# Attention interleaved with a feed-forward: two key chunks per visit, three banks for the dense products

## The chip, the cores and the metric

The kernel runs on one core of one Trainium2 chip. A core has five engines with queues of their own: TensorE (PE, matrix products into PSUM; its weight loads are listed as PEld), VectorE (DVE), ScalarE (ACT), GpSimd (POOL) and SyncE (SP), which here only issues DMA. Each queue is worked off in order; engines wait for one another through semaphores. PSUM has eight banks, and a matrix product writes into one of them until another engine has read it. The metric is the time of one execution on the device, in microseconds, the median of several runs.

## The reference

Attention with normalized queries and keys (8 batches, 12 heads, 448 positions, head width 64), then a feed-forward with squared ReLU over all 3584 tokens (width 768, inner width 2048), everything in float32:

```python
q_n, k_n = rmsnorm(q, g_q), rmsnorm(k, g_k)
scores = q_n @ k_n.T / sqrt(64)
attn = exp(scores - max);  attn = attn / (sum(attn) + 1e-9)
x = (attn @ v) rearranged to (batch * 448, 12 * 64)
h = maximum(x @ w_in, 0)
out = (h * h) @ w_out
```

## The kernel before, in words

**Attention.** Work goes by pairs of heads, 48 of them (`pairs`, six per batch). For a pair, `load_qk` and `load_v` fetch queries, keys and values, `square` (ScalarE) and `normalize` (VectorE, GpSimd) give the norms, and `turn` transposes the queries (x = 0) and keys (x = 1) on TensorE (L181) and copies them out of PSUM with VectorE or ScalarE. The keys are cut into four chunks of 112 (`NJ = 4`). `weigh(i, m)` makes the scores of chunk m for both heads (L202; one head on each half of the array's rows) and ScalarE takes the exponentials (L204). Since the exponentials are bounded, no maximum is taken off. `attend(i, m)` multiplies weights and values (L262; one head on each half of the array's columns). The denominators are products with ones: for the twelve first pairs (`alone`) a product per chunk (L269), later one product of the weights summed by GpSimd and VectorE (`add_up`, L217 and L220; the product is L273). A reciprocal (L284) and a multiplication in `finish` (L294) give the pair's output, kept in SBUF.

**Feed-forward.** It goes by units of two batches (`ffn(u)`, u = 0 to 3). Both matrix products use a form of Strassen's scheme: seven products of half-size blocks, P1 to P7, instead of eight (`PRODUCTS`, with the bank each takes, the two forms it multiplies, and whether it starts the bank). `make_x_forms` makes the sums of inputs, `make_weight_forms` and `make_sums` those of weights. A unit has four blocks. A block has two sets of first products (`first_products`, L392; seven products of six passes each), whose results are combined on VectorE (L412), passed through ReLU and square on ScalarE (L413, L414) and kept as hidden tiles; then, in `second_products`, the rows shared by the two batches (L441), sums of hidden tiles (L435), and three groups of seven second products (L458; four passes each), which VectorE adds into accumulators (L491, L475; in the first block ScalarE copies them, L489 and L473). A float32 matmul appears as two records, here called passes.

**Banks.** Four banks (4 to 7) take the feed-forward's products in turn (`roles`, `turn_roles`); a product that takes over a bank waits until the earlier one has been read. The attention has the other four; the first pair of each unit (`between`) uses some of the feed-forward's too.

**Order.** The order of every queue is written out by hand: instructions of each engine run in program order (`manual_schedule`). Pairs 0 to 11 run without feed-forward. From then on, `ffn(u - 1)` is a generator that yields after each product with a cost, and the main loop (L662 to L698) takes as many products before each chunk of attention as keep the two in proportion. A unit's first pair runs alone; the products are spread over the chunks of the eleven others. So each chunk of a pair is a *visit* of the attention between dense products: scores of chunk n for this pair, values of chunk n for the pair before.

**Weights.** They come as 64-bit words that are converted on the way, in pieces, by ScalarE (`split_words`) and VectorE (`join_words`, L569 to L581). Sixteen pieces (`early`) are converted in the first stage, the others (`late`) during the first unit's feed-forward, one per `COST_IN` of cost, tied to the products by `convert`. The finished forms are written to DRAM and loaded again for later units (`load_in`, `load_out`).

The words of the code that the change turns on are these:

```python
FIRST_ORDER = ["P1", "P5", "P6", "P4", "P3", "P7", "P2"]
SECOND_ORDER = ["P1", "P5", "P2", "P6", "P4", "P3", "P7"]
roles = list(banks[4:8])
COST_IN, COST_OUT = 12 * NK // 2, 10
```

Of the kernel before, what the change touches and what calls it, by code (L numbers as in the profile page):

```python
# [74 lines left out]
def program(ctx, tc, q, k, v, g_row, moe_w_in, moe_w_out, out, shift):  # L75
# [40 lines left out]
    weights, sums, dens, xts, forms = {}, {}, {}, {}, {}  # L116

# [3 lines left out]

    def between(i):

        return pairs[i][0] % 2 == 0 and pairs[i][1] == 0
# [50 lines left out]
    def turn(i, x):  # L175

        rows = normal[i][0][x]
        tr = banks[2 + x if alone(max(i - 1, 0)) else 2][:, 0:S]
        dst = att.tile([P, S], F32, name="qT" if x == 0 else "kT")
        for j in range(NJ):  # L180
            nc.tensor.transpose(tr[:, ts(j, CP)], rows[:, j].rearrange("p h d -> p (h d)"), ident[:CP, :CP])  # L181
        if x == 0:
            nc.vector.tensor_scalar(out=dst, in0=tr, scalar1=g, scalar2=None, op0=ALU.mult)  # L183
        else:
            nc.scalar.copy(dst, tr)  # L185
        turned[i, x] = dst

    def new_weights(i, m):
        for e in range(2):
            weights[i, e, m] = att.tile([CP, S], F32, name="wT", tag="wT", bufs=2 * NJ + 2)  # L190

    def weigh(i, m):
# [5 lines left out]
        odd = (2, 3) if alone(i) else (4, 6) if between(i) else (0, 1)  # L198
        scs = [banks[odd[e] if m % 2 else e][:CP, 0:S] for e in range(2)]
# [7 lines left out]
        add_up(i, m)  # L207

    def add_up(i, m):

        if m < 2 or alone(i):
            return
        for e in range(2):
            engine = nc.gpsimd if e == 0 else nc.vector
            if m == 2:
                sums[i, e] = att.tile([CP, S], F32, name="sum", tag="sum", bufs=2)
                engine.tensor_tensor(  # L217
                    out=sums[i, e], in0=weights[i, e, 0], in1=weights[i, e, 1], op=ALU.add
                )
            engine.tensor_tensor(out=sums[i, e], in0=sums[i, e], in1=weights[i, e, m], op=ALU.add)  # L220

    def weigh_shifted(i, m):
# [18 lines left out]
        if m == NJ - 1:  # L241
            for n in range(NJ):
                add_up(i, n)

    def values_bank(i):
        apart = i < last and between(i + 1)
        return banks[4 + i % 2 if alone(i) else 5 if apart else 3][:, 0:S]

    def sums_bank(i):
        apart = i < last and between(i + 1)  # L250
        return banks[6 + i % 2 if alone(i) else 7 if apart else 2][:, 0:S]

    def attend(i, m):

        av = values_bank(i)
        den = sums_bank(i)  # L260
# [5 lines left out]
        for e in range(2):  # L266
            wT = weights.pop((i, e, m))
            if alone(i):
                nc.tensor.matmul(  # L269
                    den[ds(e * D, D), :], lhsT=ones, rhs=wT, start=m == 0, stop=m == NJ - 1  # L270
                )
            elif m == 1:
                nc.tensor.matmul(  # L273
                    den[ds(e * D, D), :], lhsT=ones, rhs=sums.pop((i, e)), start=True, stop=True
                )
        if m == (NJ - 1 if alone(i) else 1):
            rden = new_x()
            if shift:
                nc.vector.tensor_scalar(
                    out=rden, in0=den, scalar1=1e-9, scalar2=None, op0=ALU.add  # L280
                )
                nc.vector.reciprocal(out=rden, in_=rden)
            else:
                nc.vector.reciprocal(out=rden, in_=den)  # L284
            dens[i] = rden
# [4 lines left out]
    def finish(i):  # L290
# [8 lines left out]
        if b % 2 and c >= NK:  # L299
            make_x_forms(b // 2, c - NK)  # L300
# [44 lines left out]
    roles = list(banks[4:8])  # L345

    def turn_roles(order):

        x, v_, w, y = roles
        roles[:] = (y, v_, w, x) if order is FIRST_ORDER else (w, y, v_, x)  # L350

# [3 lines left out]
        "P4": (3, True, "22", "T4"), "P5": (1, True, "S1", "T1"), "P6": (0, False, "S2", "T2"),  # L355
# [3 lines left out]
    FIRST_ORDER = ["P1", "P5", "P6", "P4", "P3", "P7", "P2"]  # L359
    SECOND_ORDER = ["P1", "P5", "P2", "P6", "P4", "P3", "P7"]  # L360
# [3 lines left out]
    def ffn(u):  # L364
# [5 lines left out]
        for blk in range(NBLK):  # L370
# [4 lines left out]
            for t in range(2):  # L375
                yield from first_products(u, 2 * blk + t, [a[:, t] for a in hid])
            yield from second_products(u, blk, hid, accs)
# [5 lines left out]
    def first_products(u, p, hid):  # L383
# [4 lines left out]
        for name in FIRST_ORDER:  # L388
# [8 lines left out]
            if name in ("P1", "P5", "P6", "P4"):  # L397
                copies[name] = ffn_p.tile([P, S], F32, name="part", tag="part", bufs=4)
                nc.scalar.copy(copies[name], ps)  # L399
            elif name == "P2":  # L400
                hidden(hid[0][:, 0], ps, copies["P1"], ALU.add)
                load_in(n + 2)
            elif name == "P3":
                hidden(hid[0][:, 1], ps, copies["P6"], ALU.add)
            elif name == "P7":
                hidden(hid[1][:, 0], ps, copies["P4"], ALU.subtract)
                hidden(hid[1][:, 1], ps, copies["P5"], ALU.add)
            yield COST_IN
        turn_roles(FIRST_ORDER)

    def hidden(dst, ps, part, op):
        nc.vector.tensor_tensor(out=dst, in0=ps, in1=part, op=op)  # L412
# [3 lines left out]
    def second_products(u, blk, hid, accs):  # L416
# [14 lines left out]
        for engine, dst, left, right, op in (  # L431
            (nc.vector, s1, a21, a22, ALU.add), (nc.vector, s2, s1, a11, ALU.subtract),
            (nc.gpsimd, s4, a12, s2, ALU.subtract), (nc.gpsimd, s3, a11, a21, ALU.subtract),
        ):
            engine.tensor_tensor(out=dst, in0=left, in1=right, op=op)  # L435

        for half in range(2):
            ps = roles[half][:, 0:HALF]
            for a in (1, 0):
                for t in range(2):  # L440
                    nc.tensor.matmul(  # L441
                        ps, lhsT=flat[a][:, t, ds(FULL, P)], rhs=w_sb[t][:, 2 * a + half, :],
                        start=a == 1 and t == 0, stop=a == 0 and t == 1,
                    )
            add_to(accs[-1][:, ts(half, HALF)], ps, blk == 0)
            yield 2 * COST_OUT
        turn_roles(SECOND_ORDER)

        lefts = {"11": a11, "12": a12, "22": a22, "S1": s1, "S2": s2, "S3": s3, "S4": s4}
        for tt in range(NT):  # L450
# [31 lines left out]
            turn_roles(SECOND_ORDER)  # L482
# [150 lines left out]
    late = deque(conversions(2, product + 2 * COST_IN, COST_IN))  # L633
    for blk in range(1, NBLK):
        late.extend(conversions(4 if blk < NBLK - 1 else 2, blk * block + 1, COST_IN))
# [15 lines left out]
    unit_steps = 2 * NPAIR * NJ  # L651

    with tc.manual_schedule(engines=ENGINES):
# [7 lines left out]
        stream, spent = iter(()), 0  # L661
        for i, (b, c) in enumerate(pairs):  # L662
            u = b // 2
            for n in range(NJ):
                step = (b % 2) * NPAIR * NJ + c * NJ + n
                if n == 0:
                    if i > 1 and not shift:
                        finish(i - 2)
                    load_v(i)
                if n == NJ - 1 and i + 3 <= last:  # L670
                    load_qk(i + 3)
                if step == NJ and u:
                    stream, spent = ffn(u - 1), 0
                while u and (
                    shift and step == NJ and spent < COST
                    or spent * (unit_steps - NJ) < COST * (step - NJ + 1)
                ):
                    spent += next(stream)
                    while u == 1 and late and late[0][0] <= spent:
                        convert(late.popleft()[1])  # L680
                if n == 2 and i + 2 <= last:
                    normalize(i + 2)
                if shift and n == 0 and i:
                    for m in range(NJ):
                        attend(i - 1, m)
                    finish(i - 1)
                weigh(i, n)
                if i and not shift:
# [49 lines left out]
```

## Time and profile before

| | |
|---|---|
| median of 3 runs | 1588.81 us (1587.44 to 1589.5) |
| profiled execution | 1587.84 us, span of its instructions 1586.0 us |
| TensorE busy | 1523.8 us, 5204 passes |
| VectorE busy | 821.0 us |
| ScalarE busy | 622.0 us |
| GpSimd busy | 454.3 us |
| mean granted TensorE clock | 0.991 |
| reciprocal, VectorE | 48, mean 2957 ns |
| exponential, ScalarE | 384, mean 628 ns |
| addition into an accumulator, VectorE | 324, mean 551 ns |

A line of the profile names an engine, a line of the kernel (L392), an operation and its tiles, out<-in. Busy time of TensorE is pipelined: a pass is listed for 543 ns while the next one starts before it ends, so times between starts are what counts. A line of the windows view gives a stretch of the span, its length, and the busy time of each engine in it. A line of the waits view says which engine at which line waited for which other, with the total, the number and the longest, in us.

### The profile page before, as it was taken

The numbers are of one execution on the slowest core, as the hardware profiler recorded it, in microseconds if no ns is written. First come the engines' busy times: TensorE is split into PE (matmuls) and PEld (weight loads), VectorE is DVE, ScalarE is ACT, GpSimd is POOL, SyncE is SP. The second block draws the span as 40 slices with busy tenths as digits, with TensorE's granted clock in tenths as the row PEclk, the third lists the DMA queues.
The fourth block names the chain that finished last, engine by engine and source line by source line (L and its number), as shares of the span: only waits on it lengthen the run. The fifth ranks groups of instructions, "written<-read, shape, count | busy, mean of one in ns | idle before, by whom it ended". The sixth has DMA issues, their size and how long they took to land.

```text
span 1586.0 us, 15000 instructions
## 1 busy us (share of the span) xinstructions
PE 1523.8 (96%) x5204; PEld 703.3 (44%) x5204; DVE 821.0 (52%) x1234; ACT 622.0 (39%) x1161; POOL 454.3 (29%) x298
## 2 busy tenths in 40 slices
PE   5999999899799999999999999999999999999997
PEld 2333444344344444444444444444444444555554
DVE  3887485977958654345363563345444452223323
ACT  4775464726527244341433334343332412231130
POOL 3445433332423353322132333223231221000000
PEclk9999999999999999999999999999999999999999
DMA  4555143533525152230313242132222205222122
GB/s 103 158 148 169 32 130 97 197 118 92 185 84 182 53 184 92 74 123 18 132 55 125 74 148 89 52 132 62 101 92 97 69 13 184 78 106 106 43 80 72
DMA packets 131801, 164.65 MB, mean 104 GB/s; under 512 B 92804, under 2 KB 115844, under 8 KB 123524
## 3 DMA queue, kind: packets, MB, share of 16 engines
q1 hardware_dynamic: 131712, 163.60, 31.6%
q8 instruction: 43, 0.70, 0.2%
q14 instruction: 42, 0.34, 0.1%
q10 hardware_dynamic: 4, 0.00, 0.0%
HBM read 128.98 MB, written 34.60 MB: 103 GB/s over the span
## 4 chain that ended last, share of the span: by engine, by line
PE 89%; DVE 5%; ACT 4%; issue 1%; POOL 0%; DMA 0%; POOLq 0%; ACTq 0%; DVEq 0%
PE bank L392 29%; PE bank L458 28%; PE bank L202 11%; PE bank L262 10%; PE bank L441 4%; PE bank L181 3%; PE bank L269 2%; PE bank L273 2%; DVE xT L284 1%; ACT hid L414 1%; ACT hid L413 1%; DVE sum L220 1%; ACT wT L204 1%; DVE hid L412 1%; DVE in_sb L607 0%
## 5 line engine op out<-in xcount | busy, mean ns | idle before, releaser
L392 PE MATMUL bank<-xT,in_sb 128*128 128x448 f32 x1344 | 522.9, 543 | 2.5 <-DVE xT L294 2.5
L204 ACT ACTIVATE wT<-bank,rr 112x448 f32<-112x448 f32 x384 | 221.3, 628 | 392.4 <-PE bank L202 386.8
L392 PEld LDWEIGHTS bank<-xT,in_sb 128*128 128x128 f32 x1344 | 249.2, 190 | 252.2 <-issue 235.3
L164 POOL TENSOR_TENSOR rr<-ms,minus_half 112x16 f32<-112x16 f32 x48 | 151.0, 3145 | 567.1 <-DVE ms L160 561.8
L458 PE MATMUL bank<-out_sb,hid 128*128 128x384 f32 x768 | 277.0, 490 | 9.0 <-DVE acc L491 9.0
L491 DVE TENSOR_TENSOR acc<-acc,bank 128x384 f32<-128x384 f32 x324 | 173.2, 551 | 186.8 <-PE bank L458 155.1
L458 PE MATMUL bank<-out_sb,sums 128*128 128x384 f32 x576 | 212.4, 491 | 0.0
L284 DVE RECIPROCAL xT<-bank 128x448 f32<-128x448 f32 x48 | 141.9, 2957 | 117.3 <-PE bank L273 99.2
L202 PE MATMUL bank<-qT,kT 64*112 64x448 f32 x768 | 199.8, 595 | 1.6 <-ACT kT L185 0.6
L458 PEld LDWEIGHTS bank<-out_sb,hid 128*128 128x128 f32 x768 | 145.2, 191 | 113.3 <-DVE acc L491 10.3
L262 PE MATMUL bank<-wT,vt 112*64 112x448 f32 x768 | 188.3, 570 | 2.9 <-DVE xT L294 2.9
L399 ACT COPY part<-bank 128x448 f32<-128x448 f32 x128 | 68.0, 531 | 255.9 <-PE bank L392 255.8
L412 DVE TENSOR_TENSOR hid<-bank,part 128x448 f32<-128x448 f32 x128 | 76.2, 616 | 174.6 <-PE bank L392 171.9
L458 PEld LDWEIGHTS bank<-out_sb,sums 128*128 128x128 f32 x576 | 105.6, 190 | 81.9 <-issue 13.4
L413 ACT ACTIVATE hid<-hid 128x448 f32<-128x448 f32 x128 | 73.3, 572 | 135.4 <-DVE hid L412 135.4
L220 DVE TENSOR_TENSOR sum<-sum,wT 112x448 f32<-112x448 f32 x72 | 65.4, 909 | 116.5 <-ACT wT L204 114.1
L435 POOL TENSOR_TENSOR sums<-hid,sums 128x768 f32<-128x768 f32 x16 | 29.3, 1829 | 298.6 <-PE bank L441 182.1
L220 POOL TENSOR_TENSOR sum<-sum,wT 112x448 f32<-112x448 f32 x72 | 86.5, 1201 | 87.1 <-ACT wT L204 83.8
L441 PE MATMUL bank<-out_sb,hid 128*128 128x384 f32 x256 | 93.2, 508 | 16.0 <-ACT hid L414 16.0
L202 PEld LDWEIGHTS bank<-qT,kT 64*112 64x112 f32 x768 | 55.6, 175 | 114.4 <-issue 58.8
L262 PEld LDWEIGHTS bank<-wT,vt 112*64 112x64 f32 x768 | 38.6, 136 | 132.1 <-issue 117.7
L183 DVE TENSOR_SCALAR qT<-bank,g 128x448 f32<-128x448 f32 x48 | 32.7, 682 | 95.8 <-PE bank L181 95.8
(53 smaller groups left out, 1084.1 us busy)
## 6 DMA issues: line engine op xcount, KB each, us to landing
out_sb<-out_forms SPq DMA_DIRECT2D x24, 1536.0 KB, 8.1
in_sb<-in_forms SPq DMA_DIRECT2D x24, 1344.0 KB, 5.7
words<-in_moe_w_in_dram SPq DMA_DIRECT2D x32, 384.0 KB, 3.6
words<-in_moe_w_out_dram SPq DMA_DIRECT2D x32, 384.0 KB, 3.2
out_forms<-out_sb SPq DMA_DIRECT2D x8, 1536.0 KB, 6.7
qk<-in_q_dram SPq DMA_DIRECT2D x96, 112.0 KB, 2.9
qk<-in_k_dram SPq DMA_DIRECT2D x96, 112.0 KB, 3.0
vt<-in_v_dram SPq DMA_DIRECT2D x48, 224.0 KB, 2.8
```

Of the source, the lines that this page charges most:

```text
L164: nc.gpsimd.tensor_tensor(out=rr.rearrange("p x r -> p (x r)"), in0=ms, in1=minus_half.to_broadcast([CP, 4 * NJ]), op=ALU.pow,)
L202: nc.tensor.matmul(sc, lhsT=kT[r, ts(m, CP)], rhs=qT[r, :], start=True, stop=True)
L204: nc.scalar.activation(weights[i, e, m], sc, AF.Exp, scale=normal[i][1][:, 2 * m + e : 2 * m + e + 1])
L220: engine.tensor_tensor(out=sums[i, e], in0=sums[i, e], in1=weights[i, e, m], op=ALU.add)
L262: nc.tensor.matmul(av[ds(e * D, D), :], lhsT=values[i][:, e, m, :], rhs=weights[i, e, m], start=m == 0, stop=m == NJ - 1,)
L284: nc.vector.reciprocal(out=rden, in_=den)
L392: nc.tensor.matmul(ps, lhsT=w_sb[:, IN.index(left), c, :], rhs=forms[u, c][right], start=first and c == 0, stop=c == NK - 1, skip_group_ch ...
L412: nc.vector.tensor_tensor(out=dst, in0=ps, in1=part, op=op)
L413: nc.scalar.activation(dst, dst, AF.Relu)
L441: nc.tensor.matmul(ps, lhsT=flat[a][:, t, ds(FULL, P)], rhs=w_sb[t][:, 2 * a + half, :], start=a == 1 and t == 0, stop=a == 0 and t == 1,)
L458: nc.tensor.matmul(ps, lhsT=lefts[left][:, t, ts(tt, P)], rhs=w_sb[t][:, OUT.index(right), :], start=first and t == 0, stop=t == 1, skip_g ...
L491: nc.vector.tensor_tensor(out=acc, in0=acc, in1=ps, op=ALU.add)
```

## The change

- A pair is visited twice instead of four times, each time for two chunks: in the first visit of pair i the values of pair i - 1 for chunks 0 and 1 and the scores of pair i for chunks 0 and 1, in the second the rest. The values come first now. The denominators' product stands at the start of the second visit and is copied out of PSUM by ScalarE; the reciprocal then works on the copy in SBUF. Scores take banks 0 to 3.
- The transposes of `turn` stand halfway between two visits, in bank 0. In the stage before the feed-forward they take, of the two banks each that values and denominators have in turn, those not in use.
- VectorE's work for the attention (reciprocal, `finish`, sums, norms) goes into a list, `tasks`, of which one is issued after each product.
- The feed-forward has three banks (5 to 7) instead of four. The orders of the products are new; P4 comes last in the first products, and P7's copy is taken from PSUM and P4 subtracted from it.
- The shared rows are multiplied in two parts: three of the four factors for both halves, then the sums of hidden tiles are issued, then the last factor.
- All twelve pairs of a unit, its first one included, are spread over the feed-forward of the unit before, in 24 equal steps: the scores of the next unit's first pair are made in the last steps. The x forms are made when those of the unit before have been used (`complete`). In the old order the last pair's values came after the last spread product; now they are spread too.
- Late conversions come every `2 * COST_OUT` (20) instead of every `COST_IN` (18). The weights' buffers are 8 instead of 10, those of the sums 4 instead of 2.

```diff
@@ def turn
-        tr = banks[2 + x if alone(max(i - 1, 0)) else 2][:, 0:S]
+        tr = banks[6 - 2 * x + (i - 1) % 2 if i < 2 or alone(i - 2) else 0][:, 0:S]
@@ def weigh
-        odd = (2, 3) if alone(i) else (4, 6) if between(i) else (0, 1)
-        scs = [banks[odd[e] if m % 2 else e][:CP, 0:S] for e in range(2)]
+        scs = [banks[m % 2 * 2 + e][:CP, 0:S] for e in range(2)]
...
-        add_up(i, m)
@@ instead of the end of attend
+    def denominators(i):
+        den = sums_bank(i)
+        for e in range(2):
+            nc.tensor.matmul(
+                den[ds(e * D, D), :], lhsT=ones, rhs=sums.pop((i, e)), start=True, stop=True
+            )
+        dens[i] = new_x()
+        nc.scalar.copy(dens[i], den)
+
+    def invert(i):
...
+        nc.vector.reciprocal(out=dens[i], in_=den)
@@ feed-forward
-    roles = list(banks[4:8])
+    roles = list(banks[5:8])
...
-        "P4": (3, True, "22", "T4"), "P5": (1, True, "S1", "T1"), "P6": (0, False, "S2", "T2"),
+        "P4": (2, True, "22", "T4"), "P5": (1, True, "S1", "T1"), "P6": (0, False, "S2", "T2"),
...
-    FIRST_ORDER = ["P1", "P5", "P6", "P4", "P3", "P7", "P2"]
-    SECOND_ORDER = ["P1", "P5", "P2", "P6", "P4", "P3", "P7"]
+    FIRST_ORDER = ["P1", "P5", "P2", "P6", "P3", "P7", "P4"]
+    SECOND_ORDER = ["P1", "P2", "P5", "P6", "P3", "P4", "P7"]
@@ def first_products
-            if name in ("P1", "P5", "P6", "P4"):
+            if name in ("P1", "P5", "P6", "P7"):
...
-                hidden(hid[1][:, 0], ps, copies["P4"], ALU.subtract)
                 hidden(hid[1][:, 1], ps, copies["P5"], ALU.add)
+            elif name == "P4":
+                hidden(hid[1][:, 0], copies["P7"], ps, ALU.subtract)
+                load_in(n + 2)
@@ def second_products
+        parts = [(0, 0), (1, 0), (0, 1), (1, 1)]
+        for some in (parts[:3], parts[3:]):
+            for half in range(2):
+                ps = roles[half][:, 0:HALF]
+                for a, t in some:
                     nc.tensor.matmul(
                         ps, lhsT=flat[a][:, t, ds(FULL, P)], rhs=w_sb[t][:, 2 * a + half, :],
-                        start=a == 1 and t == 0, stop=a == 0 and t == 1,
+                        start=(a, t) == parts[0], stop=(a, t) == parts[-1],
                     )
...
+            if some[-1] != parts[-1]:
+                for engine, dst, left, right, op in (
+                    (nc.vector, s1, a21, a22, ALU.add), (nc.vector, s2, s1, a11, ALU.subtract),
+                    (nc.gpsimd, s4, a12, s2, ALU.subtract), (nc.gpsimd, s3, a11, a21, ALU.subtract),
+                ):
+                    engine.tensor_tensor(out=dst, in0=left, in1=right, op=op)
@@ order
+    def run(until):
+        nonlocal spent
+        while spent < until:
+            spent += next(stream)
+            while first and late and late[0][0] <= spent:
+                convert(late.popleft()[1])
+            if complete and (complete[0][0] - 1, complete[0][1]) not in forms:
+                make_x_forms(*complete.popleft())
+            if tasks:
+                tasks.popleft()()
...
+    def visit(i, n):
+        chunks = range(2 * n, 2 * n + 2)
+        if i and not shift:
+            if n and not alone(i - 1):
+                denominators(i - 1)
+            for m in chunks:
+                attend(i - 1, m)
...
+    def visit_among(i, n):
+        while tasks:
+            tasks.popleft()()
+        visit(i, n)
+        if i <= last:
+            weigh_chunks(i, n)
+        if n and not shift:
+            tasks.append(lambda: invert(i - 1))
+            tasks.append(lambda: finish(i - 1))
+        if i <= last and not shift:
+            for m in range(2 * n or 1, 2 * n + 2):
+                add_up(i, 0, m)
+                tasks.append(lambda m=m: add_up(i, 1, m))
+        if n == 0 and i + 2 <= last:
+            square(i + 2)
+            tasks.append(lambda: None)
+            tasks.append(lambda: normalize(i + 2))
...
+        for i in range(len(pairs) + 1):
+            for n in range(VISITS):
+                at = i * VISITS + n - VISITS - unit
+                if at < 0:
+                    visit_alone(i, n)
+                    continue
...
+                run(COST * (2 * x - 1) / (2 * unit))
+                if i < last:
+                    turn(i + 1, n)
+                    if n and i + 3 <= last:
+                        load_qk(i + 3)
+                run(COST * x / unit)
+                if x == unit:
+                    drain()
+                    stream, spent, first = ffn(u + 1), 0, u < 0
+                visit_among(i, n)
```

## The prediction

> **What bounds the kernel now.** I read the page's busy times and its chain of waits first:
>
> ```profile
> PE 1523.8 (96%) x5204; PEld 703.3 (44%) x5204; DVE 821.0 (52%) x1234; ACT 622.0 (39%) x1161; POOL 454.3 (29%) x298
> ...
> PE 89%; DVE 5%; ACT 4%; issue 1%; POOL 0%; DMA 0%; POOLq 0%; ACTq 0%; DVEq 0%
> ```
>
> TensorE sets the end; only 10% of the chain is other engines. A busy TensorE can still be filled with overhead, so I cut the span at the first matmul of each unit's feed-forward (FFN 0 to 3), the view by stages:
>
> ```profile
> 15.30:165.20 149.90, 145.84 (x705) 51.19 (x705) 106.47 (x157) 102.83 (x194) 69.81 (x40) 1.00 0.50 143
> 165.20:572.90 407.70, 381.69 (x1266) 173.34 (x1264) 294.28 (x458) 199.91 (x386) 140.04 (x97) 0.98 0.38 124
> 572.90:946.90 374.00, 371.98 (x1266) 170.60 (x1264) 172.10 (x245) 132.98 (x243) 115.44 (x74) 1.00 0.28 93
> 946.90:1318.30 371.40, 367.23 (x1234) 168.46 (x1232) 166.75 (x235) 124.59 (x227) 107.34 (x70) 1.00 0.26 88
> 1318.30:1586.00 267.70, 256.65 (x738) 139.41 (x736) 79.14 (x134) 59.21 (x110) 16.98 (x10) 0.99 0.24 88
> ```
>
> The columns after the length are busy PE, PEld, DVE, ACT, POOL, clock, DMA share, GB/s. FFN 0 does FFN 1's work plus the weight conversions, and takes 33.7 us longer: VectorE is busy 294 us there against 172. The last stage is dense matmuls alone. Its chain gives the price of one pass:
>
> ```profile
> 1382.87 29.33 PE bank L392 x78
> ...
> 1447.13 29.33 PE bank L392 x78
> ```
>
> 29.33/78 = 0.376 us per 448-column pass, and 64.26 us per block of feed-forward without attention. Next the timeline of TensorE with attention mixed in:
>
> ```profile
> 1072.84 4.69 PE L392 MATMUL bank<-xT,in_sb 128*128 128x448 f32 x12
> 1077.45 1.01 PE L202 MATMUL bank<-qT,kT 64*112 64x448 f32 x4
> 1078.39 0.97 PE L262 MATMUL bank<-wT,vt 112*64 112x448 f32 x4
> 1079.30 2.52 PE L392 MATMUL bank<-xT,in_sb 128*128 128x448 f32 x6
> 1081.66 2.10 PE L441 MATMUL bank<-out_sb,hid 128*128 128x384 f32 x6
> ```
>
> The visit's 8 passes run two at a time on half arrays, so they need 4 x 0.376 = 1.50 us; start to start they take 1.85. The 12 passes before take 4.61 instead of 4.51, the 6 after 2.36 instead of 2.26. So one visit wastes 0.35 + 0.10 + 0.10 = 0.55 us (0.54 used) in three changes of shape: full to half rows, half rows to half columns, and back to full. Last, the waits of TensorE on others:
>
> ```profile
> PE bank L441 <- ACT hid L414: 16.0, 14, 4.5
> ...
> PE bank L458 <- DVE acc L491: 9.0, 2, 6.3
> ```
>
> Total us, times, longest. They are the shared rows waiting for the last hidden tile, and an accumulator bank not yet read, nearly all of it in FFN 0.
>
> **What the Trainium skill says.** "TensorEngine Tiling (Array Packing)", Tiling Modes: changing the tiling mode drains TensorE. The 0.1 us at each change agrees. "PSUM — Partial Sum Buffer", the section on bank collisions: engines must be kept apart by bank; so a product that takes a bank over waits for its last reader, which makes three banks instead of four a matter of slack. "VectorE: DVE Perf Modes", The fixed hardware budget: reciprocal is an iterative divide; the trace has 2957 ns beside 615 for the multiply of the same shape, so I keep 2.96 us when its source moves from PSUM to SBUF. "GPSIMD Engine Reference", Specifications: GpSimd shares SBUF interfaces with VectorE instructions with two SBUF inputs. Agrees: the L607 addition on VectorE took 0.55 us usually and 4.45 at 422.76, beside GpSimd work.
>
> **The change, part by part** (per-pass prices as above).
>
> *Half the visits.* The 36 pairs after pair 11 had 4 visits each: 132 among dense products (0.54 each) and 12 in the three first pairs of a unit, without dense products (two changes, about 0.37). That is 75.7 us of changes. Now 72 visits, again with three changes each (denominators and values are the same shape, then scores, then dense): 72 x 0.54 = 38.9. Gain 36.8. The passes themselves stay: eight score, eight value and two denominator matmuls per pair.
>
> *Turns apart.* The transposes now stand between dense products, half a visit away. They cost 0.35 us inside a visit (2.29 against 1.85, less the dearer return of 0.09); alone 4 x 0.096 = 0.38 plus at most 0.08 of entry: +0.03 to +0.11 for 72, I take 5 us in all. SP's loads of q and k wait behind these transposes; they have over one visit's interval (15 us) before their squares, against 2.9 us to landing.
>
> *The stage before FFN.* One pair takes 11.29 us (transposes 68.86 to 80.15), TensorE always busy, eight changes for the four chunks. Pairs of chunks need about five instead: 0.56 less for 12 pairs, 7 us. ScalarE carries 9.2 us per pair of 10.7 with the conversions; its exponentials stand ahead of squares and conversions, so I charge no wait. Half a visit (3.2 us) moves here from later, which is neutral.
>
> *First pair of a unit, last pair.* The attention of the next first pair is spread as the others. The old end of FFN 2, 1308.4 (last dense pass) to 1318.3, is 9.9 us for 4.5 us of passes: 5.4 gained.
>
> *Shared rows last.* The factor made last is needed after 6 matmuls (12 passes of 0.323 = 3.9 us) and, by the new order, after a visit (4.3 us) too. Its chain is 0.64 + 0.59 + 0.58 us and gaps, 2.0. The L441 wait goes unless VectorE lags 6 us.
>
> *Waits that go.* Taking start-to-start gaps over the normal ones, I count 33.5 us in FFN 0, 2.5 in each of FFN 1 and 2, 0.7 in FFN 3: 39. All are set to zero here, and what VectorE costs now is added next.
>
> *Three banks.* In first products the shortest slack stays one product (2.26 us, P6 to P7); ScalarE's burst after a visit, four exponentials and two squares, ends some 2.6 us after it, before that product needs its copy. In second products P5 frees its bank for P3 within one product (1.29 us), all others within two or three (2.58, 3.87). Six visits fall on each block at fixed places. The reciprocal now queues behind the additions of P7 in the second third: P7's two additions end at 2.4 us after the visit, the reciprocal at 5.3, P1's addition 5.8, finish 6.35, P2's 6.85, a sum 7.4, P5's 7.9. P6 could start at 5.75 and P3 at 7.2; they start at 5.9 and 8.0. Stall 0.9 us; 2.1 in the last block, where x forms stand between, plus 0.5 around its shared rows. In the first block ScalarE takes most of these readings. 4.4 us per unit, 9 in FFN 1 and 2. The copy of the denominators ahead (0.53 us ScalarE) is done by 2.5 us into the visit; the score that reuses its bank starts at 3.3. GpSimd's sums keep their place at the visit; only VectorE's are spread.
>
> *FFN 0.* VectorE's work in the second and third block was 81.0 of 102.6 and 83.9 of 108.4 us. Undisturbed, a block would take TensorE now 256/4 + 104.9/4 = 90 us (12 pairs: 24 visits, denominators and turns, 8.74 us a pair). 84 us in order, with lumps of 2.2 to 2.8 us, cannot all hide in 90: a conversion falls on every second product at the start of the second products (one per 20 cost units, 10 a product). Counting on as above, with 2.75 us per conversion, additions come 3 to 5 us late there, and P3 twice waits 3 to 4 us for its bank. I take 11 us for each of these blocks, 5 for the first and last together: 27.
>
> Sum: 36.8 - 5 + 7 + 5.4 + 39 - 9 - 27 = 47. Span 1586.0 - 47 = 1539; by stages 162 + 387 + 366 + 357 + 267. The profiled execution took 1587.84, 1.84 more than its span, and the median is 0.97 over that: **1542 us**.
>
> Ends of the unknown terms: FFN 0 costs 10 us (all hidden but dependencies) to 45 (three banks stop at every lump); reciprocals 0 to 25; turns 2 to 8; the stage before FFN -7 to +5.
>
> **Rivals.** *Conversions give most back:* FFN 0 costs 45 instead of 27 and the reciprocals 15: 1566. For it: VectorE at 93% of a block; against: the old stalls came mostly from the order of the shared rows, which is mended. *All hidden:* VectorE finds its 6 us per block, 1515 to 1528. Against: the addition of P5 has 1.29 us and a reciprocal takes 2.96. *Slower:* in second products of FFN 0 to 2 the bank of P5 stalls in every group of seven, not once a block. There are 36 such groups beside attention (3 in each of 12 blocks); from 47/36 = 1.3 us each the gain is gone, and at 2 us the time is 1542 + 72 = 1614. For it: the slack is one product, 1.29 us. Against: in groups without a reciprocal or conversion an addition ends 0.6 us after its product. *The visits get no cheaper:* if the waste belongs to each weight load and not to the change of shape, 36.8 and 7 drop out of the sum and 1542 + 44 = 1586, no change. Against: passes of one shape that follow each other do not show it.
>
> **How the numbers follow.** Likeliest, 1528 to 1555: 0.55. Given back, 1555 to 1585: 0.20. All hidden, below 1528: 0.12. Slower: 0.10. Within 0.2% (3 us, what a measurement of this kernel tells from no change): 0.03. Cutting the ends to leave two in ten, 1524 to 1573. Faster 0.87.
>
> **What would show it.** Visits of 16 passes with the same 0.55 us of waste; TensorE's matmul count unchanged; FFN 1 at 366 instead of 374; L441 waits under 3 us in all; additions waiting in the middle blocks of FFN 0; L392 right behind the end of FFN 2. It is wrong if TensorE's waits on accumulator additions exceed 60 us, if the copy of the denominators holds the scores up, or if the stage before FFN 0 gets longer.

## The result, and the profile after

The changed kernel takes 1598.46 us (median of 4 runs, 1597.25 to 1599.35); the kernel before took 1588.74 beside it. The ratio is 1.0062 with a 95% interval of 1.0044 to 1.0079: slower, where 1542 us and "faster" had been forecast. The profiled execution has a span of 1597.0 us, 58 more than the 1539 of the sum.

Busy times and shares of the chain of work that ended last, from the page of the kernel after:

```profile
PE 1508.5 (94%) x5204; PEld 733.1 (46%) x5204; DVE 845.9 (53%) x1234; ACT 632.9 (40%) x1197; POOL 450.1 (28%) x298
...
PE 81%; DVE 13%; ACT 2%; issue 2%; POOL 0%; SPq 0%; DMA 0%; ACTq 0%; DVEq 0%; POOLq 0%
```

TensorE is busy 15.3 us less than before, in spite of more time at half clock: the visits did get cheaper. But VectorE, 5% of the chain before, is now 13%. The view by stages, with the columns as before (length, then busy PE, PEld, DVE, ACT, POOL, clock):

```profile
15.30:167.40 152.10, 144.74 (x724) 56.91 (x724) 118.61 (x159) 102.88 (x196) 70.63 (x42) 0.99 0.49 144
167.40:594.90 427.50, 387.09 (x1266) 184.91 (x1264) 294.27 (x464) 204.20 (x400) 150.05 (x103) 0.96 0.35 112
594.90:969.50 374.60, 366.04 (x1266) 178.28 (x1264) 181.62 (x244) 135.74 (x256) 113.45 (x74) 0.99 0.28 93
969.50:1332.00 362.50, 354.84 (x1214) 172.99 (x1213) 171.96 (x227) 126.88 (x238) 97.86 (x65) 0.99 0.26 88
1332.00:1597.00 265.00, 255.44 (x737) 139.65 (x735) 77.07 (x132) 60.65 (x110) 14.31 (x8) 0.99 0.28 100
```

Against the forecast by stages (162, 387, 366, 357, 267) the miss is +5.4, **+40.5**, +8.6, +5.5 and -2.0, together 58. FFN 0, the unit with the conversions, carries most of it: 427.5 us, where before it took 407.7. Against the kernel before, FFN 0 loses 19.8 us and the stage ahead of it 2.2; FFN 2 and the last stage win 8.9 and 2.7. VectorE's busy time in FFN 0 did not change (294.28 before, 294.27 now); what changed is who waits for it, and what it waits for. From the waits of the kernel after (us in all, times, longest):

```profile
DVE hid L403 <- ACT part L389: 117.1, 35, 6.4
...
PE bank L452 <- DVE acc L485: 34.9, 20, 4.8
...
PE bank L178 <- POOL qk L166: 17.4, 3, 11.7
...
PE bank L198 <- ACT xT L263: 9.0, 6, 2.9
...
PE bank L382 <- ACT part L389: 7.1, 3, 2.4
```

The waits of the shared rows, 16.0 us before, are gone as forecast. In their place TensorE waits for accumulators (34.9 us, 9.0 before), for the copy of the denominators (L263) and for ScalarE's copies in the first products (L389). Within FFN 0 these waits of TensorE add up to 40.0 us (19.5 + 9.0 + 7.1, and 3.3 + 1.1 for finished tiles and a transposed q); before it was 26.1. VectorE itself waits for ScalarE's copies of products (L403 for L389), in FFN 0 for 29.0 us in 11 waits; the kernel before had no such wait there. The only wait for a DMA in FFN 0 is ScalarE's for weight words, 3.2 us in three, so the fewer weight buffers do not show as a cause. The clock in FFN 0 fell from 0.98 to 0.96 as well.

One of these waits, in the timeline of VectorE, ScalarE and TensorE (start, us, engine and line; lines between are left out at the dots):

```profile
297.37 1.76 PE L198 MATMUL bank<-qT,kT 64*112 64x448 f32 x8
...
299.06 4.78 PE L382 MATMUL bank<-xT,in_sb 128*128 128x448 f32 x12
...
299.45 0.56 DVE L571 SCALAR_TENSOR_TENSOR out_sb<-words,out_sb 128x384 uint32<-128x384 uint32 x1
...
300.14 0.56 DVE L575 CUSTOM_DVE_ANT_0 out_sb<-words,out_sb 128x768 uint16<-128x768 uint16 x1
300.62 0.62 DVE L212 TENSOR_TENSOR sum<-sum,wT 112x448 f32<-112x448 f32 x1
301.15 0.62 DVE L403 TENSOR_TENSOR hid<-bank,part 128x448 f32<-128x448 f32 x1
...
301.80 0.58 ACT L404 ACTIVATE hid<-hid 128x448 f32<-128x448 f32 x1 [1.37 <-DVE hid L403]
...
302.41 0.58 ACT L405 ACTIVATE hid<-hid 128x448 f32<-128x448 f32 x1
...
302.90 2.19 ACT L200 ACTIVATE wT<-bank,rr 112x448 f32<-112x448 f32 x4
...
304.96 1.16 ACT L148 ACTIVATE squares<-qk 112x512 f32<-112x512 f32 x2
...
306.00 0.54 ACT L389 COPY part<-bank 128x448 f32<-128x448 f32 x1
...
306.59 6.26 PE L382 MATMUL bank<-xT,in_sb 128*128 128x448 f32 x12 [2.37 <-ACT part L389]
```

VectorE's addition for P2 (301.15) stands behind a conversion and a sum of weights. ScalarE, which works in order, waits 1.37 us for it with the Relu; the four exponentials of the visit that ended at 299.06, the squares and then the copy of P6 stand behind that Relu. P7 takes over P6's bank, so TensorE stands for 2.37 us, and then runs at half speed. Blocks 1 to 3 of FFN 0 have one such wait each, the 7.1 us of L382 above. The view by windows of the 3 us after the restart and of the next 3 (clock is the third number from the end):

```profile
306.60:309.60 3.00, 3.00 (x4) 1.50 (x5) 2.93 (x5) 2.94 (x7) 1.56 (x2) 0.50 0.12 41
309.60:312.60 3.00, 3.00 (x9) 1.33 (x7) 1.67 (x4) 2.28 (x5) 0.00 (x0) 1.00 0.26 73
```

Four passes instead of nine. The Trainium skill, "TensorE: Matmul & The Clock Gate", What's actually happening, describes a half-rate clock after an idle window of about 3.4 us and the same time of work to leave it. The trace agrees with the half rate and roughly with its length, 3.0 us of work; the idle stretch was shorter here, 2.37 us. Not every stretch of that length is followed by a slow one: after a wait of 2.76 us that ends at 331.43 the clock stays at 1.00.

```profile
331.50:334.50 3.00, 2.19 (x6) 1.09 (x7) 3.00 (x3) 0.00 (x0) 3.00 (x2) 1.00 0.99 421
```

In FFN 1 and FFN 2 the waits sit in the last block, where the forms of x are made; here that of FFN 1:

```profile
914.78 3.69 POOL L311 TENSOR_TENSOR xT<-xT 128x448 f32<-128x448 f32 x2
...
917.87 5.28 DVE L311 TENSOR_TENSOR xT<-xT 128x448 f32<-128x448 f32 x2
918.43 1.81 POOL L440 TENSOR_TENSOR sums<-hid,sums 128x768 f32<-128x768 f32 x1
...
920.19 1.80 POOL L440 TENSOR_TENSOR hid<-hid 128x768 f32<-128x768 f32 x1
...
924.53 0.54 DVE L485 TENSOR_TENSOR acc<-acc,bank 128x384 f32<-128x384 f32 x1
...
925.13 6.96 PE L452 MATMUL bank<-out_sb,sums 128*128 128x384 f32 x12 [4.65 <-DVE acc L485]
```

The first of VectorE's two L311 operations began at 917.87 and took 4.62 us, against a median of 0.625 for all 24: it ended only when GpSimd had got through three operations in a row. The accumulator's addition, behind it and a sum of weights, came at 924.53, and TensorE stood for 4.65 us. The last blocks of FFN 0 and FFN 2 have the same, one such operation of 4.62 and 4.61 us.

### The profile page after: what moved, and what is told of

Its sections match the earlier page's. It is cut to its first block, busy times and chain, and to the rows that moved or that the text cites. A ratio compares the mean times of both kernels' runs of the same rounds, so it can differ in the third digit from the quotient of the medians.

```text
span 1597.0 us, 14972 instructions
## 1 busy us (share of the span) xinstructions
PE 1508.5 (94%) x5204; PEld 733.1 (46%) x5204; DVE 845.9 (53%) x1234; ACT 632.9 (40%) x1197; POOL 450.1 (28%) x298
## 4 chain that ended last, share of the span: by engine, by line
PE 81%; DVE 13%; ACT 2%; issue 2%; POOL 0%; SPq 0%; DMA 0%; ACTq 0%; DVEq 0%; POOLq 0%
PE bank L382 29%; PE bank L452 24%; PE bank L198 10%; PE bank L244 9%; PE bank L428 4%; DVE xT L274 3%; PE bank L251 2%; PE bank L178 2%; DVE acc L485 2%; PE bank L259 2%; DVE sum L212 1%; DVE xT L311 1%; DVE sums L440 1%; DVE hid L403 1%; DVE in_sb L567 1%
## 5 line engine op out<-in xcount | busy, mean ns | idle before, releaser
L382 PE MATMUL bank<-xT,in_sb 128*128 128x448 f32 x1344 | 526.7, 546 | 7.1 <-ACT part L389 7.1
L382 PEld LDWEIGHTS bank<-xT,in_sb 128*128 128x128 f32 x1344 | 251.6, 192 | 258.1 <-issue 244.8
L200 ACT ACTIVATE wT<-bank,rr 112x448 f32<-112x448 f32 x384 | 211.9, 634 | 339.5 <-PE bank L198 338.3
L452 PE MATMUL bank<-out_sb,hid 128*128 128x384 f32 x768 | 268.2, 495 | 5.5 <-DVE acc L485 5.5
L403 DVE TENSOR_TENSOR hid<-bank,part 128x448 f32<-128x448 f32 x96 | 59.9, 624 | 307.2 <-PE bank L382 178.6
L161 POOL TENSOR_TENSOR rr<-ms,minus_half 112x16 f32<-112x16 f32 x48 | 140.1, 2918 | 267.4 <-DVE ms L157 246.4
L198 PE MATMUL bank<-qT,kT 64*112 64x448 f32 x768 | 179.5, 571 | 10.7 <-ACT xT L263 9.0
L244 PE MATMUL bank<-wT,vt 112*64 112x448 f32 x768 | 169.7, 552 | 3.3 <-DVE xT L283 3.3
L212 POOL TENSOR_TENSOR sum<-wT 112x448 f32<-112x448 f32 x36 | 40.9, 1136 | 379.8 <-ACT wT L200 379.8
L389 ACT COPY part<-bank 128x448 f32<-128x448 f32 x128 | 67.9, 530 | 151.8 <-PE bank L382 151.8
L212 POOL TENSOR_TENSOR sum<-sum,wT 112x448 f32<-112x448 f32 x72 | 83.0, 1153 | 110.1 <-ACT wT L200 107.2
L274 DVE RECIPROCAL xT<-xT 128x448 f32<-128x448 f32 x36 | 106.1, 2946 | 11.4 <-ACT xT L263 11.4
L244 PEld LDWEIGHTS bank<-wT,vt 112*64 112x64 f32 x768 | 50.2, 137 | 97.1 <-issue 81.1
L428 PE MATMUL bank<-out_sb,hid 128*128 128x384 f32 x256 | 91.6, 514 | 0.0
L212 DVE TENSOR_TENSOR sum<-wT 112x448 f32<-112x448 f32 x36 | 37.5, 1041 | 96.3 <-ACT wT L200 96.3
```

What stands on the lines that cost most here:

```text
L161: nc.gpsimd.tensor_tensor(out=rr.rearrange("p x r -> p (x r)"), in0=ms, in1=minus_half.to_broadcast([CP, 4 * NJ]), op=ALU.pow,)
L198: nc.tensor.matmul(sc, lhsT=kT[r, ts(m, CP)], rhs=qT[r, :], start=True, stop=True)
L200: nc.scalar.activation(weights[i, e, m], sc, AF.Exp, scale=normal[i][1][:, 2 * m + e : 2 * m + e + 1])
L212: engine.tensor_tensor(out=sums[i, e], in0=left, in1=weights[i, e, m], op=ALU.add)
L244: nc.tensor.matmul(av[ds(e * D, D), :], lhsT=values[i][:, e, m, :], rhs=weights[i, e, m], start=m == 0, stop=m == NJ - 1,)
L274: nc.vector.reciprocal(out=dens[i], in_=den)
```

## The experiments

All were timed side by side with the kernel before, which took 1587.63 to 1588.21 us beside them. "FFN 0" is from the first matmul of that unit's feed-forward to the first of the next. Its blocks are numbered 0 to 3; the time of a block's first products is from its first matmul to its shared rows.

| kernel | time, us | ratio to before, 95% | FFN 0, us |
|---|---|---|---|
| before | 1588.7 | | 407.7 |
| after | 1598.5 | 1.0062 (1.0044 to 1.0079) | 427.5 |
| feed-forward part alone | 1598.5 | 1.0070 (1.0048 to 1.0092) | 412.6 |
| before, shared rows' order alone | 1584.3 | 0.9977 (0.9965 to 0.9988) | 408.0 |
| before, light conversions | 1568.1 | 0.9868 (0.9851 to 0.9884) | 390.5 |
| after, light conversions | 1564.7 | 0.9866 (0.9841 to 0.9892) | 392.7 |
| after, forms of x later | 1587.0 | 0.9988 (0.9978 to 0.9999) | 423.7 |
| after, conversions every 25 | 1590.2 | 1.0019 (1.0011 to 1.0026) | 423.7 |
| after, both of these | 1578.4 | 0.9948 (0.9931 to 0.9965) | 416.9 |
| after, Relu later | 1583.7 | 0.9976 (0.9969 to 0.9983) | 414.3 |
| after, P7's tile from copies | 1579.2 | 0.9953 (0.9937 to 0.9969) | 410.5 |
| after, first three edits | 1560.1 | 0.9835 (0.9813 to 0.9858) | 398.0 |
| after, all four edits | 1557.1 | 0.9804 (0.9788 to 0.9821) | 399.8 |
| before's visits, feed-forward part with the last two edits | 1591.0 | 1.0022 (1.0015 to 1.0029) | 407.0 |

**The forms of x.** They are issued only at a product that has no other task:

```diff
-            if complete and (complete[0][0] - 1, complete[0][1]) not in forms:
-                make_x_forms(*complete.popleft())
             if tasks:
                 tasks.popleft()()
+            elif complete and (complete[0][0] - 1, complete[0][1]) not in forms:
+                make_x_forms(*complete.popleft())
```

> The x forms of the next unit are issued only at a product that has no other task, so after GpSimd's sums of hidden tiles instead of beside them. Theory 1 (the x forms on VectorE are held up while GpSimd works on those sums, which costs TensorE 11 us in the last block of each unit, its lower clock afterwards included): FFN 1 from 374.6 to about 364, FFN 2 from 362.5 to about 354, FFN 0 down by 10; in all about 1598 - 28 = 1570 us, and no subtraction of an x form over 2 us on VectorE. Rival (three banks stall at any lump of VectorE work, wherever it stands): the stalls move with the forms and the time stays within 5 us of 1598.

Measured 1587.0, 11.5 us less, between the two expectations (28 less, or within 5). The last block of FFN 0, 1 and 2 fell from 108.5, 102.4 and 90.2 us to 104.6, 96.3 and 89.7. The group of VectorE's operations, of the kernel after and then of this one (ns: shortest, median, longest):

```profile
L311 DVE TENSOR_TENSOR xT<-xT x24: 616/625/4616, 164.3 to 1326.9; 128x448 f32<-128x448 f32 x24
```

```profile
L311 DVE TENSOR_TENSOR xT<-xT x24: 609/625/1584, 163.1 to 1315.2; 128x448 f32<-128x448 f32 x24
```

None of these operations is over 2 us any more, so the meeting with GpSimd's sums is the cause of the 4.62 us. Not all of the block's loss was this meeting: one wait of 3.41 us for an accumulator remains at 921.59, behind the moved operations.

**The pace of the conversions.** One every 25 cost units instead of 20 (`2 * COST_OUT` becomes `25`):

> Late conversions come every 25 units of cost instead of every 20, so that they spread over the whole block of 502 instead of its first 400. Theory 2 (in FFN 0 the conversions come in faster than VectorE can take them beside the rest, though the block as a whole has room: 81 us busy of 110): FFN 0 falls by 15 to 25 us, the rest stays, 1573 to 1583 us. Rival (each conversion is a lump that three banks cannot bear, however far apart): FFN 0 within 5 us of 427.5, about 1595 us.

1590.2, 8.3 less, but FFN 0 fell by 3.8 only, within the 5 of the rival, and the first products of blocks 1 and 2 stayed at 54.7 and 54.1 us. Block 0 won 4.7 us (97.5 to 92.8), block 3 lost 1.6 (108.5 to 110.1); the rest came in small pieces elsewhere, 1.5 in FFN 1. Density of conversions is not what hurts the first products.

**Both together.**

> Both edits of the two runs before. If both theories hold and the two losses are separate: 1598 - 28 - 20 = 1550 us, below the kernel before. If both rivals hold: 1590 to 1598.

1578.4, which is short of the 1550 hoped for, but already beats both kernels: 20.1 us off the changed one, where the two edits alone gave 11.5 and 8.3. They add up, so they are two separate losses.

**The feed-forward part alone**: the kernel before with three banks, the new product orders and the new order of shared rows, but the old visits of one chunk.

> The kernel before with the feed-forward of the changed kernel alone: three banks, its product orders and the order of the shared rows; attention, visits and conversions as before. If three banks hurt only where the conversions load VectorE: FFN 1 and FFN 2 within 3 us of before (374.0 and 371.4), FFN 0 up by 5 to 20 from 407.7, in all 1590 to 1608 us. Rival (three banks cost time everywhere): FFN 1 up by 10 us or more, in all over 1620 us. If the new order of the shared rows gains more than three banks lose: below 1585.

1598.5, as slow as the whole change, but by another way. Its FFN 0 is only 4.9 us longer than before, its FFN 1 and FFN 2 are 2.0 and 1.5 longer, as the first expectation had it; and 3.4 us more lie ahead of FFN 0, where its very first product waits 4.45 us for a finished tile of the attention. In its FFN 0 the first products take 45.2, 44.5, 46.4 and 45.0 us per block, where the whole change takes 49.6, 55.0, 55.0 and 52.1. The slow first products thus need the attention's part of the change too. That this means its two-chunk visits is argued from the timeline; its other pieces, such as the new places of VectorE's tasks, were not tried apart.

**The order of the shared rows alone**, on the kernel before with its four banks:

```diff
...
-            for a in (1, 0):
-                for t in range(2):
+        parts = [(1, 0), (1, 1), (0, 0), (0, 1)]
+        for some in (parts[:3], parts[3:]):
+            for half in range(2):
+                for a, t in some:
...
```

> The kernel before, four banks, with one part of the change: the factor that is made last comes last in the shared rows. The forecast took the 16.0 us of waits of the shared rows as gone. If they go, with the slow restarts behind them, 1567 to 1576. If VectorE and ScalarE are merely met late at the next bank, 1582 to 1589, with the waits of the second products on accumulators up from 9.0 us.

Waits of this kernel:

```profile
PE bank L460 <- DVE acc L493: 24.0, 4, 12.4
...
PE bank L442 <- ACT hid L414: 3.6, 7, 1.4
```

The shared rows' wait fell from 16.0 to 3.6 us, and the wait on accumulators rose from 9.0 to 24.0. FFN 0 did not get shorter (408.0 against 407.7); the 3.7 us that the kernel won lie in FFN 1 and FFN 2. In the timeline of block 2 the kernel before waits 1.40 and 3.37 us at the shared rows and 6.33 at the second products, and goes on at 433.11; this one waits 1.31 and 12.44, and goes on here:

```profile
421.23 1.72 POOL L609 TENSOR_TENSOR in_sb<-in_sb 128x384 f32<-128x384 f32 x1
422.00 4.88 DVE L609 TENSOR_TENSOR in_sb<-in_sb 128x384 f32<-128x384 f32 x1
422.90 1.80 POOL L435 TENSOR_TENSOR sums<-hid,sums 128x768 f32<-128x768 f32 x1
424.67 1.79 POOL L435 TENSOR_TENSOR hid<-hid 128x768 f32<-128x768 f32 x1
...
434.32 1.01 PE L460 MATMUL bank<-out_sb,hid 128*128 128x384 f32 x1 [12.44 <-DVE acc L493]
```

It is the same meeting with GpSimd (0.55 us of work taking 4.88), here in a weight sum of the old kernel. TensorE came to the late accumulator earlier and waited longer.

**Light conversions**, on the changed kernel and on the one before. They leave out three of VectorE's four operations of each late conversion; only the shift is left:

```diff
+            if n >= 16:
+                nc.vector.tensor_scalar(
+                    out=bits, in0=high, scalar1=4, scalar2=1,
+                    op0=ALU.logical_shift_left, op1=ALU.logical_shift_right,
+                )
+                if form == 3:
+                    make_weight_forms(kind, targets.pop((kind, t)), t)
+                return
```

> The changed kernel, but of the four VectorE operations of each of the 48 conversions beside the feed-forward only the shift is left (min/max, and/or, add left out, so about 1.47 of 1.83 us each, 70 us in all). Theory B: FFN 0 falls from 427 us to about 395, the time to 1565 to 1570. Theory A: it also falls, since nothing makes VectorE late any more, by about the same; if it stays above 1585, the loss is ScalarE's own load or the order of the products, and neither theory holds.

> The kernel before, with only the shift left of the four VectorE operations of each of the 48 conversions beside the feed-forward (min/max, and/or, add left out). The same edit took 33.7 us from the changed kernel. If the change made the conversions dearer (three banks, two chunks per visit), this takes clearly less here, 15 to 25 us (1563 to 1573), and FFN 0 falls from 407.7 to 383 to 393 us. If the conversions cost both kernels the same, it takes 30 us or more, below 1559.

FFN 0 of the changed kernel and of the kernel before, both with light conversions:

```profile
165.50:558.20 392.70, 374.60 (x1266) 180.37 (x1264) 236.71 (x367) 203.17 (x400) 147.79 (x103) 0.98 0.38 122
```

```profile
164.70:555.20 390.50, 378.98 (x1266) 173.24 (x1264) 237.84 (x362) 199.48 (x386) 138.88 (x97) 0.98 0.40 130
```

The same work came off VectorE in both, 57.6 and 56.4 us (less than the 70 that the expectation worked out). It shortened FFN 0 by 34.8 us in the changed kernel and by 17.2 in the one before. The change made the same conversions twice as dear. As both theories had expected this fall, it does not tell them apart.

**Relu and square issued after the next product's copy**, so that no copy stands right behind a Relu that waits for VectorE:

```diff
         nc.vector.tensor_tensor(out=dst, in0=left, in1=right, op=op)
-        nc.scalar.activation(dst, dst, AF.Relu)
-        nc.scalar.activation(dst, dst, AF.Square)
+        made.append(dst)
+
+    made = deque()
+
+    def square_made():
+        while made:
+            dst = made.popleft()
+            nc.scalar.activation(dst, dst, AF.Relu)
+            nc.scalar.activation(dst, dst, AF.Square)
...
                 nc.scalar.copy(copies[name], ps)
+                square_made()
...
                 hidden(hid[1][:, 0], copies["P7"], ps, ALU.subtract)
+                square_made()
```

> The changed kernel, but the two ScalarE operations that finish a hidden tile (Relu, square) are issued after the next product's copy instead of right behind VectorE's addition. Theory A (ScalarE's queue): in the new order the copy of P6 stands behind the Relu of P2, which waits for VectorE's addition, which waits behind conversions; so TensorE waits for copies and restarts at half clock. Then the first products of blocks 1 to 3 of FFN 0 fall from 55.0, 55.0 and 52.1 us to below 49, and the time from 1598 to 1575 to 1588. Theory B (VectorE has too much in FFN 0, whatever the order on ScalarE): first products stay above 53, the time within 4 us of 1598.

1583.7, 14.8 less. First products of blocks 1 to 3 fell to 52.8, 52.6 and 46.4 us, only in the last below the 49 expected. TensorE's 7.1 us of waits on copies in the first products are gone altogether; its waits for the copy of the denominators rose from 9.0 to 10.7. Theory A names a real cause, but not all of it; B, which expected no gain, falls.

**P7's tile one product later, from copies:**

```diff
-            elif name == "P7":
-                hidden(hid[1][:, 1], ps, copies["P5"], ALU.add)
             elif name == "P4":
+                hidden(hid[1][:, 1], copies["P7"], copies["P5"], ALU.add)
                 hidden(hid[1][:, 0], copies["P7"], ps, ALU.subtract)
```

> The changed kernel, but P7's hidden tile is added one product later, from the SBUF copies of P7 and P5, so that VectorE never reads the bank that ScalarE copies. Theory C (two readers of P7): VectorE's 117 us of waits on that copy are lateness, and go; first products of FFN 0 fall by 4 us or more per block and the time to 1580 to 1588. Theories A and B: those waits are mostly waits for the product itself, VectorE has slack there, and the time stays within 5 us of 1598.

1579.2, 19.3 less. The line of this kernel that answers to the 117.1 us:

```profile
DVE hid L402 <- ACT part L389: 44.9, 29, 2.1
```

Most of the 117.1 us lies where it costs nothing; in FFN 0 these waits fell from 29.0 to 3.5 us. There, reading P7's bank after ScalarE's copy made VectorE stand idle with conversions queued behind it. The first products of blocks 1 to 3 fell to 51.7, 51.5 and 47.5; the 4 us per block that theory C expected came in the last alone, and the time was just below its range.

**Three and four edits together.**

> The changed kernel with three edits: the x forms issued at a product with no other task, a conversion every 25 cost units instead of 20, and Relu and square after the next copy. The first two together gave 1578.4. Theory A: 12 to 22 us less, 1557 to 1567, first products of FFN 0 below 49 us in every block. Theory B: 1575 to 1580.

> The kernel of three edits (1560.1) with the fourth as well: P7's hidden tile added one product later, from SBUF copies. If the late Relu and the two readers of P7 are two separate losses, their gains add as measured alone (14.8 and 19.3 us off 1598.5), and the time falls by another 10 to 15, to 1545 to 1550. If both only give back the same lateness of VectorE and ScalarE, it stays at 1556 to 1561.

The Relu edit on top of the first two gives 18.3 us more (1560.1), with first products below 49 us in every block, as theory A had it. P7's tile on top of that gives only 3.0, far from the 19.3 that it gave alone: the last two edits give back the same lateness. With all four the change is worth 1.96% against the kernel before. The stages of the fastest kernel, FFN 0 and then, for its FFN 1, one of the undisturbed blocks:

```profile
165.50:565.30 399.80, 375.42 (x1267) 180.56 (x1265) 290.64 (x463) 203.48 (x400) 148.17 (x103) 0.97 0.38 120
```

```profile
746.00:837.00 91.00, 90.44 (x318) 44.04 (x316) 44.92 (x63) 32.11 (x62) 26.01 (x17) 1.00 0.27 89
```

FFN 1 and 2 of that kernel take 366.1 and 358.5 us (first matmul to first matmul), within 1.5 us of the forecast's 366 and 357.

**The last two edits with the old visits**, that is, in the kernel of the feed-forward part alone:

> The kernel before with the feed-forward part of the change (1598.5), and the late Relu and P7's tile from copies, old visits of one chunk. If the order on ScalarE and VectorE alone made that part slower, it falls to 1580 to 1588. If these orders only hurt together with visits of two chunks, whose four exponentials, copy and squares make ScalarE late, it stays at 1592 to 1600: first products in its FFN 0 took only 44.5 to 46.4 us per block.

1591.0, between the two expectations: 7.5 us less than without the edits. Its first products (45.2, 43.2, 47.0, 44.1) were hardly slow to begin with. So the new orders account for part of what that kernel loses. With the old attention part the two edits give 7.5 us, in the changed kernel one of them alone gives 14.8 or 19.3.

## Why the prediction was wrong

**The visits: right.** The 16 passes of a visit waste the same 0.55 us, and the three undisturbed blocks of FFN 1 take 89.7, 91.3 and 91.3 us in the kernel after, where 90 had been worked out. With a fourth like them the unit would take 363.6, where the forecast had 366. In the stage before, one pair takes 10.76 us instead of 11.29, 0.53 less, where 0.56 was forecast. The last stage took 265.0 us, where 267 was forecast.

**"FFN 0 ... 27": the step that failed.** The undisturbed unit takes 363.6, FFN 0 427.5: 63.9 us for conversions, forms of x and what they set off, beyond the 45 of the range's far end. About 40 of it are waits, and about 17 the clock, (1 - 0.96) x 427.5; the forecast worked out stalls in the second products of the middle blocks only, took 5 us for the other two blocks, and counted no slow restarts. The sentence that ScalarE's burst "ends some 2.6 us after it, before that product needs its copy" (after the visit) holds where VectorE is on time: in FFN 1 the visit ending at 775.91 has its burst done at 778.54. With conversions ahead of it VectorE's addition is late, the Relu holds up ScalarE, and the burst starts late: in the timeline above it ends at 306.12, 7.1 us after the visit. I checked each engine's slack alone, not the chain of VectorE, Relu, copy and bank that the new order builds; the old order had its four copies ahead of the first addition. Relu later, P7's tile from copies, and light conversions each shorten that chain or take away its cause, and took 13.2, 17.0 and 34.8 us out of FFN 0.

**"Waits that go ... 39": not safe to set to zero.** The run with the shared rows' order alone shows it: 12.4 us of waits taken away at one place, 15.0 added at the next, FFN 0 unchanged. TensorE ran into the same late VectorE one step on. The order of shared rows was right as a local reading (the wait went), and worth 3.7 us of time.

**The forms of x: mis-sized.** I charged 2.1 - 0.9 = 1.2 us for them in the second products and 0.5 beside the shared rows. The last block shows 102.4 us in FFN 1 against 91.3, so about 11. I had cited the line with 4.45 us beside GpSimd work and did not ask where the change would bring the two together again. The Trainium skill, "SBUF — State Buffer", SBUF: two separate sides, says that a VectorE operation with two SBUF inputs and a GpSimd operation that reads SBUF exclude each other for a whole instruction. The trace agrees, and shows more: the loser waited through three GpSimd operations in a row. Moving the forms brought FFN 1 to 368.5.

**Copy of the denominators: "done by 2.5 us", not in FFN 0.** The scores waited 9.0 us for it there, none elsewhere. The stall at accumulators in every group of seven, the slower rival, is not what happened: in each middle block of FFN 1 and FFN 2 TensorE waits once, for 0.43 us, where 0.9 had been worked out. The rival had the right direction by the wrong mechanism. Of the three signs of being wrong, two came, the copy of the denominators and a longer stage before FFN 0; the third did not, since the waits on accumulators are 34.9 us and not over 60.

**The stage before FFN 0: 167.4 instead of 162.** TensorE's waits for normalized q and k (L166) rose from 13.5 to 17.4 us: 11.7 instead of 10.7 at the start, and a new one of 2.96 us that ends at 161.93, where GpSimd's power operation (2.90 us) and multiply come too late for the transposes of the last pair. That is 3.9 of the 5.4; the 1.0 at the start belongs to this one execution, since in the profiles of all eight kernels made from it that wait is 10.4 to 10.7 us. The half clock after the new wait (0.94 in the last 27 us, 1.00 before the change) is worth 1.6 more by (1 - 0.94) x 27. I had charged no wait there.

**Still open.** The attention's part alone was not run, since two chunks of scores need banks that only the three-bank feed-forward leaves. FFN 0 of the fastest kernel is still 33.7 us longer than its FFN 1; 16.7 us of it are waits for accumulators, and what would remove these was not tried.

## What to carry to other kernels

A wait that ends in a late engine is not a gain when it is removed: ask where TensorE meets that engine next, and try the part alone. When an order of products is changed, follow the chain through all engines' queues (here an addition on VectorE, a Relu in front of a copy on ScalarE, a bank on TensorE) with the late engine's lateness put in, not each engine's slack on its own. Price a stall of TensorE with the slow restart that can follow it: in the kernel after, of its 16 stalls of 1.8 to 4.8 us behind the start-up, 14 had a stretch of half clock begin during them or within 2 us. It is no certainty: stalls of 3.30 and 3.13 us in the kernel of four edits had none.

## What the runs showed of the hardware

- A VectorE operation on two SBUF operands beside GpSimd took 4.62 us (median 0.625), and 4.88 in another kernel. Both times it ended 0.4 to 0.5 us after the last of three back-to-back GpSimd operations, not after the first.
- TensorE ran at half clock for 3.0 us after a wait of 2.37 us, and at a mean clock of 0.58 from 925.1 to 931.9 us after one of 4.65. After waits of 2.76 us there, and of 3.30 us in the kernel of four edits, the clock stayed at 1.00.
